# State term on 64x64 tiles, packed states, scores between two psH blocks and a new order, in a fused attention and MLP kernel

## The chip, the cores and the metric

The kernel runs on one NeuronCore of one Trainium2 chip. The metric is the device time of one execution in microseconds (us). A run of the kernel before on the same chip stands beside every run. Where several times are given they are a median, with the lowest and the highest in brackets. A run is called slow when its matmuls ran at a lower pace or it lies over 1.5% above the fastest run of the same kernel; such runs are left out of the ratios.

## The reference

Linear attention with decay, in blocks, then an MLP with ELU. The kernel works on 128 tokens at a time, so 24 blocks ("groups") of 4 sequences by 6 chunks, and computes in f16 with f32 sums.

```python
# q, k, v: (4 sequences, 8 heads, 768 positions, 64); per block of positions:
intra = (q_b @ k_b.T * Dmask) @ v_b              # "scores" S, then the product P with v
inter = (q_b * lam_pow) @ kv_state               # the state term
out_b = intra + inter
kv_state = lam_block * kv_state + (k_b * rev_pow).T @ v_b    # product U, then the update
# x = out as (3072 tokens, 512); w_in (512, 2048), w_out (2048, 512)
h = x @ w_in                                     # first product, psH
g = where(h > 0, h, exp(min(h, 0)) - 1)
y = g @ w_out                                    # second product, psM
```

## The kernel before

Groups 0 to 3 are worked on one by one, the others in pairs. From pair 8 on, the second product is done in seven products of half size in place of eight (a Strassen scheme). It needs sums of neighbouring quarters of g: `fp` (128x512), `fe` (128x256) and `fd` (128x512), and at the end combinations of the seven results (`t`, `u`, `s2`, `w1`). A table says which of the sums go to GpSimd; those are issued at once, the others are queued for VectorE:

```python
SHARED = {8: 'D', 10: 'ED', 12: 'ED', 14: 'ED', 16: '', 18: '', 20: '', 22: 'ED'}
...
for w, out, in0, in1, op in (
    ("P", p, t[:, :, 0], t[:, :, 1], ALU.add),
    ("E", e, t[:, :, 0, 0], t[:, :, 1, 1], ALU.add),
    ("D", d, t[:, :, :, 1], t[:, :, :, 0], ALU.subtract),
):
    if w in SHARED.get(g0, ""):
        nc.gpsimd.tensor_tensor(out=out[:], in0=in0, in1=in1, op=op)
    else:
        todo.append(lambda ...: nc.vector.tensor_tensor(...))
```

In the timelines below every engine works through its instructions in program order (TensorE waits 2.66 us for `pp` with a psM block behind it in its order). Each psH block ends in a "flush", which issues VectorE's `gg` (the last step of g), then one waiting attention piece (`late`, for instance `pp`, the masked scores), then one waiting sum (`slow`):

```python
if late:
    late.pop(0)()
if slow and len(late) < 2:
    slow.pop(0)()
```

The order of a pair is given by a table of positions, counted in psH blocks from the pair's first one: loads of q, k, v (`L`), transposes (`T`), scores (`S`), and the burst of attention products (`B`). GpSimd issues the loads, and its work stands in its own program order: load issues, `fe`, `fd`, `t`, `kd` (the keys with their decay).

```python
AT = {'L': -19, 'l': 1, 'W': -13, 'T': -5, 'S': -7, 'B': -5}
```

Of the kernel before, what the change touches and what calls it, by code (L numbers as in the profile page):

```python
# [15 lines left out]
def kernel(  # L16
# [27 lines left out]
    WI = [2] * 8  # L44
    WO = [2] * 8
    POOL_ORDER = (
        "q1 k0 iota k2 k1 q2 v0 v1 i0 i1 v2 i3 i2 o0 o1 d0 k3 q3 i4 i5 d1 o2 d2 o3 d3 o4 v3 o5 "
        "i6 i7 k4 o7 o6 q4 k6 m4 v4 q6 d5 d4 q8 q10 k8 d6 v6 v8 d7 v10 k10 m6"
# [4 lines left out]
        "z3 z0 z1 Z2 Z1 z2 Z0 T0 T1 S0 S1 T2 P0 P1 S2 1:0:0 U0 1:1:0 P2 1:1:1 1:2:0 2:0:0 "  # L53
        "1:2:1 2:1:0 1:0:1 T3 2:2:0 1:0:2 S3 1:2:2 2:2:1 U1 1:1:2 2:1:1 2:0:1 P3 2:0:2 1:3:0 "
        "2:1:2 1:1:3 M 1:2:3 Z3 2:2:2 1:3:2 U2 1:3:1 2:1:3 1:0:3 T4 T5 2:2:3 1:3:3 S4:5 2:3:0 "
        "2:0:3 2:3:2 U3 F0 B:P4:P5:U4:U5 M 2:3:3 1:4:1 T6 1:4:0 G3 T7 2:3:1 G4 W9 1:4:3 G5 G1 "
        "S6:7 1:4:2 G2 2:5:0 2:4:0 1:4:4 1:4:5 W8 B:P6:P7:U6:U7 1:4:7 1:6:1 2:5:1 2:4:1 G7 "
        "1:4:6 1:6:0 G6 2:4:2 S8:9 1:6:2 1:6:4 2:5:2 2:5:3 W11 1:6:3 1:6:6 B:P8:P9:U8:U9 1:6:7 "
        "2:4:3 1:6:5 W10 L12"
    )  # L60
    LAGU = 13
    LATE = 4
    MACT = 12
    SPLIT = 3
    DELAY = 0
    COMB = nc.gpsimd

    SEVEN = (8, 10, 12, 14, 16, 18, 20, 22)
    SHARED = {8: 'D', 10: 'ED', 12: 'ED', 14: 'ED', 16: '', 18: '', 20: '', 22: 'ED'}
    AT = {'L': -19, 'l': 1, 'W': -13, 'T': -5, 'S': -7, 'B': -5}  # L70
    BANKS = (
        "S0=M0,A S1=D,C S2=D,M1 S3=D,B P0=M1 P1=M0 P2=B P3=A U0=B U1=B U2=B U3=M1 T0=M1,D "
        "T1=D,C T2=M0,D T3=B T4=B T5=D T6=M1 T7=D M2=C M3=M0"
# [19 lines left out]

    stp = [
        [cpool.tile([128, 2, NHP, 128], FP16, name=f"st{x}_{i}") for i in range(2)]
# [5 lines left out]
    def emit_load(w, g0):  # L101
        n = size_of[g0]
        c, b = divmod(g0, B)
        x = {"q": q, "k": k, "v": v}[w]
        src = x[b : b + n, :, c * L : (c + 1) * L].rearrange("b h p d -> p (b h) d")
        t = asb.tile([128, n, H, 64], FP16, tag=f"{w}n{n}", name=f"{w}n{g0}", bufs=4)
        {"q": qg, "k": kg, "v": vg}[w][g0] = t
        nc.gpsimd.dma_start(out=t[:].rearrange("p b h d -> p (b h) d"), in_=src)  # L108
# [38 lines left out]
    def emit_wi(i):  # L147
        written.add(("i", i))
        f0 = sum(WI[:i]) * 128
        nc.gpsimd.dma_start(  # L150
            out=wi16[i][:],
            in_=moe_w_in[:, f0 : f0 + WI[i] * 128].rearrange("(k p) f -> p k f", p=128),
        )
# [48 lines left out]
    def zero_st1(b):  # L202
        nc.vector.memset(st[b][1], 0.0)

# [8 lines left out]

    dn = cpool.tile([128, H], FP32, name="dn")
    mask = cpool.tile([128, H, 128], FP32, name="mask")
    qs = cpool.tile([128, NHP, 128], FP32, name="qs")
    ks = cpool.tile([128, H], FP32, name="ks")
# [11 lines left out]
    for hh in range(2):  # L229
        r = slice(hh * 64, (hh + 1) * 64)  # L230
        nc.vector.tensor_copy(loglam_p[r, :], loglam[r, hh::2])
    nc.vector.tensor_scalar_add(pos[:, 2:3], pos[:, 1:2], float(L))

    def emit_qs():
        for hp in range(NHP):
            nc.scalar.activation(
                qs[:, hp, :], row[:], AF.Exp, scale=loglam_p[:, hp : hp + 1]
            )
# [90 lines left out]

    def att_P(g):  # L330
        cb, b = divmod(g, B)
        until(E_done, g)
        if cb > 0:
            until(Y_done, g - B)
        vt = of(vg, g)
        qt, _ = qkT[g]
        po = bank(f"P{g}", 0, [128, NHP, 128], FP32, f"psO{g}")
        R = [slice(0, 64), slice(64, 128)]
        for hp in range(NHP):
            for hh, r in enumerate(R):  # L340
                nc.tensor.matmul(  # L341
                    po[r, hp, :], lhsT=vt[:, 2 * hp + hh, :], rhs=Pt[(g, hh)][:, hp, :],
                    start=True, stop=(cb == 0), skip_group_check=True,
                )
            if cb > 0:
                for r in R:
                    nc.tensor.matmul(  # L347
                        po[r, hp, :], lhsT=st[b][cb % 2][:, hp, r], rhs=qt[:, hp, :],
                        start=False, stop=True, skip_group_check=True,
                    )  # L350

        def evacuate():
            g0 = GFIRST[g]
            n = GSIZE[g0]
            if g0 not in xg:
                xg[g0] = asb.tile(
                    [128, NHP, n * 128], FP16, tag=f"xt{n}", name=f"xt{g0}",
                    bufs=4 if n == 1 else 2,
                )
            dst = xg[g0][:, :, (g - g0) * 128 : (g - g0 + 1) * 128]  # L360
            if g < GPE:
                nc.scalar.copy(out=dst, in_=po[:])
            else:
                nc.vector.tensor_tensor(out=dst, in0=po[:], in1=qs[:], op=ALU.mult)
            X_done.add(g)

        return [evacuate]

    stt = {}

    def att_M(g):

        cb, b = divmod(g, B)
        if cb == NCB - 1 or b % 2:
            return
        assert {f"U{g - B}", f"U{g - B + 1}"} <= seen
        until(Y_done, g - B)
        until(Y_done, g - B + 1)
        old = stp[b // 2][cb % 2]
        tmp = asb.tile([128, 2, NHP, 128], FP32, tag="stt", name=f"stt{g}", bufs=2)  # L380
        stt[g] = tmp
        if g >= MACT:
            for hp in range(NHP):
                nc.scalar.activation(
                    tmp[:, :, hp, :], old[:, :, hp, :], AF.Copy, scale=upp[:, hp : hp + 1]
                )
            return
        for hh in range(2):
            r = slice(hh * 64, (hh + 1) * 64)
            for x in range(2):  # L390
                nc.gpsimd.tensor_tensor(
                    out=tmp[r, x, :, r], in0=old[r, x, :, r],
                    in1=upp[r].unsqueeze(2).broadcast_to([64, NHP, 64]), op=ALU.mult,
                )
# [5 lines left out]
    def att_U(g, pu=None):  # L400
# [5 lines left out]
        if pu is None:  # L406
            full = bank(f"U{g}", 0, [128, NHP, 128], FP32, f"psU{g}")
            for hp in range(NHP):
                nc.tensor.matmul(
                    full[:, hp, :].rearrange("p (h e) -> p h e", h=2),  # L410
                    lhsT=kds[g][:, 2 * hp : 2 * hp + 2, :],
                    rhs=vt[:, 2 * hp : 2 * hp + 2, :], start=True, stop=True,
                )
        else:
            for hp in range(NHP):
                for hh in range(2):
                    r = slice(hh * 64, (hh + 1) * 64)
                    nc.tensor.matmul(
                        pu[r, hp, :], lhsT=kds[g][:, 2 * hp + hh, :], rhs=vt[:, 2 * hp + hh, :],
                        start=True, stop=True, skip_group_check=True,  # L420
                    )
# [4 lines left out]
        def update(hh):  # L426
            r = slice(hh * 64, (hh + 1) * 64)
            nc.vector.tensor_copy(new[r, :, r], full[r, :, r])
            if hh == 1:
                Y_done.add(g)  # L430
# [3 lines left out]
    def updates(g, pu):  # L434
# [4 lines left out]
        def update(hh):  # L439
            r = slice(hh * 64, (hh + 1) * 64)  # L440
            nc.vector.tensor_tensor(
                out=new[r, :, :, r], in0=stt[g][r, :, :, r], in1=pu[r], op=ALU.add
            )
            if hh == 1:
                Y_done.update((g, g + 1))

        return [lambda: update(0), lambda: update(1)]

    def burst(*ops):

        us = [int(o[1:]) for o in ops if o[0] == "U" and int(o[1:]) // B < NCB - 1]
        evs, i = [], 0
        for o in ops:
            if o[0] == "P":
                evs += att_P(int(o[1:]))
# [67 lines left out]
    def mm2_seven(g0, i):  # L523
# [6 lines left out]
        while slow and i in (2, 4, 5):  # L530
            slow.pop(0)()
# [4 lines left out]
        while i == 6 and "w1" not in z:  # L536
            late.pop(0)()
# [102 lines left out]
        elif m == 1:  # L640
            late.insert(0, lambda: comb("w1", "u", None, ALU.add, nc.vector))
# [10 lines left out]
    def flush():  # L652
        while pending:
# [19 lines left out]
            if g0 in SEVEN and j % 2 == 1:  # L673
                slow.extend(sums(g0, j // 2))
        if late:
            late.pop(0)()
        if slow and len(late) < 2:
            slow.pop(0)()
# [64 lines left out]
    def zero_st(b):  # L743
        nc.scalar.memzero(st[b][0])

# [8 lines left out]
    def ready(t):  # L754
# [4 lines left out]
        if t[0] == "U" and g < 2 * B:  # L759
            assert f"{'z' if g < B else 'Z'}{g % B}" in seen  # L760
# [4 lines left out]
    def run(t):  # L765
# [11 lines left out]
        if w in "PUzZ":  # L777
            ready(t)
        if w == "S":
# [4 lines left out]
            late.pop(0)()  # L784
            late.pop(0)()
# [6 lines left out]
        else:  # L792
            {"T": att_T_pe, "1": mm1, "2": mm2, "Z": zero_st, "z": zero_st1,
             "q": lambda g, e: cast_raw(g, "q", e), "k": lambda g, e: cast_raw(g, "k", e),
             "7": mm2_seven, "F": w_sums, "G": lambda i: w_sums(i, nc.gpsimd), "c": lambda i: (emit_qs, emit_mask, emit_ks)[i](), "W": pool_work,
# [94 lines left out]
```

## Time and profile before

| | before |
|---|---|
| time | 212.09 us (212.03 to 213.15) |
| span of the profiled run | 210.7 us |
| TensorE, VectorE, ScalarE, GpSimd busy | 195.4, 159.0, 138.0, 159.9 us |
| one pair, 96 to 158 us | 15.50 us |

The columns of a line of the costliest groups are the source line, engine and operation, output and input, count, then the busy time in us and the mean of one in ns, and the idle time ahead of it.

```profile
L501 DVE TENSOR_TENSOR fp<-gg 128x512 f16<-128x512 f16 x32 | 14.6, 455 | 0.6
```

The 32 `fp` sums on VectorE take 0.46 us each on average, 0.70 at most.

### The profile page before, as it was taken

What the parts mean: (1) busy time and instruction counts of PE and PEld (TensorE: products, weight loads), DVE (VectorE), ACT (ScalarE), POOL (GpSimd) and SP (SyncE); (2) the same over time, 40 slices, a digit from 0 to 9 for tenths busy, and PEclk for the clock granted to TensorE, in tenths of its full rate; (3) what the DMA queues carried; (4) which work ended last, traced back from release to release, by engine and by line L of the source; (5) the groups of instructions that cost most, each with busy time, mean ns of one, the idle gap of its engine ahead of it and who ended that gap; (6) DMA issues with size and microseconds to landing.
All of it is one profiled execution on the core that took longest, in us unless ns stands there. A gap on an engine that the chain in (4) does not pass through costs nothing.

```text
span 210.7 us, 5654 instructions
## 1 busy us (share of the span) xinstructions
PE 195.4 (93%) x2224; PEld 156.4 (74%) x2224; DVE 159.0 (75%) x294; ACT 138.0 (65%) x277; POOL 159.9 (76%) x187
## 2 busy tenths in 40 slices
PE   0687999999999999999999999999999999999993
PEld 0366776767676776767887887887988888888882
DVE  3774572689956878889979879879989889886632
ACT  4537664874877675867966967867567667667640
POOL 7999799999999999497999999996370301205961
PEclk9999999999999999999999999999999999999999
DMA  7999999999993030999949969979999911011032
GB/s 86 133 165 193 194 195 186 164 184 188 135 179 83 3 100 4 133 165 150 129 88 153 120 99 153 116 93 154 153 79 180 106 51 52 3 50 50 3 121 78
DMA packets 102122, 24.61 MB, mean 117 GB/s; under 512 B 92624, under 2 KB 99280, under 8 KB 102096
## 3 DMA queue, kind: packets, MB, share of 16 engines
q0 software_dynamic: 79760, 13.50, 83.5%
q1 hardware_dynamic: 22336, 10.76, 27.1%
q8 instruction: 17, 0.28, 0.5%
q14 instruction: 9, 0.07, 0.2%
HBM read 27.27 MB, written 6.29 MB: 159 GB/s over the span
## 4 chain that ended last, share of the span: by engine, by line
PE 66%; DVE 9%; POOL 8%; ACT 7%; DMA 4%; issue 3%; ACTq 0%; POOLq 0%; DVEq 0%
PE psH L700 30%; PE psM L567 18%; PE psM L725 11%; DMA wo<-in_moe_w_out_dram 4%; ACT e L706 3%; ACT psH L707 3%; DVE gg L666 3%; PE psS L305 3%; PE psO L341 2%; DVE g L666 2%; PE psO L347 1%; POOL wi L150 1%; POOL fe L498 1%; POOL vn L108 1%; POOL kn L108 1%
## 5 line engine op out<-in xcount | busy, mean ns | idle before, releaser
L700 PE MATMUL psH<-xt,wi 128*128 128x256 f16 (+1 forms) x896 | 99.6, 258 | 2.9 <-DVE gg L666 1.3
L700 PEld LDWEIGHTS <-wi 128*128 128x128 f16 x896 | 77.8, 98 | 17.8 <-issue 4.3
L706 ACT ACTIVATE e<-psH 128x512 f32<-128x512 f32 x96 | 57.3, 597 | 47.0 <-PE psH L700 46.0
L707 ACT ACTIVATE psH<-psH 128x512 f32<-128x512 f32 x96 | 57.0, 593 | 0.0
L666 DVE SCALAR_TENSOR_TENSOR gg<-e,psH 128x512 f16<-128x512 f32 x64 | 43.7, 682 | 15.8 <-ACT psH L707 15.5
L666 DVE SCALAR_TENSOR_TENSOR g<-e,psH 128x512 f16<-128x512 f32 x32 | 21.9, 684 | 17.7 <-ACT psH L707 17.5
L321 DVE TENSOR_TENSOR pp<-psS,mask 128x512 f16<-128x512 f32 x48 | 31.4, 683 | 4.0 <-PE psS L305 4.0
L725 PE MATMUL psM<-wo,g 128*128 128x512 f16 x128 | 32.1, 379 | 0.4 <-DMA wo<-in_moe_w_out_dram 0.3
L498 POOL TENSOR_TENSOR fd<-gg 128x512 f16<-128x512 f16 x20 | 24.3, 1215 | 0.1
L177 POOL TENSOR_TENSOR kd<-kn,ks 128x512 f16<-128x512 f16 x20 | 21.1, 1057 | 4.2 <-DMA kn<-in_k_dram 4.1
L518 POOL TENSOR_TENSOR wf<-wo 128x256 f16<-128x256 f16 (+1 forms) x28 | 21.1, 789 | 0.2
L498 POOL TENSOR_TENSOR fe<-gg 128x256 f16<-128x256 f16 x16 | 11.7, 729 | 12.2 <-DVE gg L666 12.1
L620 POOL TENSOR_TENSOR t<-m,m 128x256 f32<-128x256 f32 x8 | 5.9, 734 | 18.1 <-ACT m L553 18.1
L725 PEld LDWEIGHTS <-g 128*128 128x128 f16 x128 | 11.7, 98 | 10.3 <-issue 0.8
L567 PE MATMUL psM<-wf,gg 128*128 128x256 f16 x128 | 16.7, 273 | 0.1
L567 PE MATMUL psM<-wo,fp 128*128 128x256 f16 x128 | 16.5, 273 | 0.0
L567 PE MATMUL psM<-wf,fd 128*128 128x256 f16 x128 | 16.4, 273 | 0.0
L108 POOL DMA_DIRECT2D qn<-in_q_dram x13 | 14.7, 1135 | 0.9 <-POOLq L874 0.8
L108 POOL DMA_DIRECT2D kn<-in_k_dram x14 | 15.4, 1098 | 0.0
L108 POOL DMA_DIRECT2D vn<-in_v_dram x14 | 15.3, 1099 | 0.0
L501 DVE TENSOR_TENSOR fp<-gg 128x512 f16<-128x512 f16 x32 | 14.6, 455 | 0.6
L567 PEld LDWEIGHTS <-gg 128*128 128x128 f16 x128 | 11.9, 98 | 2.3 <-DVE gg L666 0.4
(62 smaller groups left out, 249.4 us busy)
## 6 DMA issues: line engine op xcount, KB each, us to landing
out_dram<-osb SPq DMA_DIRECT2D x22, 256.0 KB, 2.7
kn<-in_k_dram POOLq DMA_DIRECT2D x10, 256.0 KB, 6.5
qn<-in_q_dram POOLq DMA_DIRECT2D x10, 256.0 KB, 6.3
vn<-in_v_dram POOLq DMA_DIRECT2D x10, 256.0 KB, 8.3
wi<-in_moe_w_in_dram POOLq DMA_DIRECT2D x8, 256.0 KB, 7.5
wo<-in_moe_w_out_dram POOLq DMA_DIRECT2D x8, 256.0 KB, 8.9
kn<-in_k_dram POOLq DMA_DIRECT2D x4, 128.0 KB, 4.5
vn<-in_v_dram POOLq DMA_DIRECT2D x4, 128.0 KB, 5.7
```

Source lines behind the costliest of these rows:

```text
L108: nc.gpsimd.dma_start(out=t[:].rearrange("p b h d -> p (b h) d"), in_=src)
L177: nc.gpsimd.tensor_tensor(out=kd[:], in0=of(kg, g), in1=ks[:].unsqueeze(2).broadcast_to([128, H, 64]), op=ALU.mult,)
L321: nc.vector.tensor_tensor(out=P[:], in0=pts[hh][:], in1=mask[:, hh::2, :], op=ALU.mult)
L498: nc.gpsimd.tensor_tensor(out=out[:], in0=in0, in1=in1, op=op)
L501: lambda out=out, in0=in0, in1=in1, op=op: nc.vector.tensor_tensor(out=out[:], in0=in0, in1=in1, op=op)
L518: eng.tensor_tensor(out=out, in0=in0, in1=in1, op=op)
L567: nc.tensor.matmul(place_of(m), lhsT=lhs, rhs=rhs, start=(s == 0 and m in (3, 4, 1, 7)), stop=(s == NFT // 2 - 1), skip_group_check=True,)
L666: nc.vector.scalar_tensor_tensor(out=g.rearrange("p f c t -> p (f c t)"), in0=e[:], scalar=-1.0, in1=r[:], op0=ALU.add, op1=ALU.min,)
L700: nc.tensor.matmul(pH[:, f * n * 128 : (f + 1) * n * 128], lhsT=wi16[i][:, kk, w * 128 : (w + 1) * 128], rhs=xg[g0][:, kk, :], start=(kk = ...
L706: nc.scalar.activation(e[:], pH[:], AF.Exp)
L707: nc.scalar.activation(pH[:], pH[:], AF.Relu)
L725: nc.tensor.matmul(psM[g][:, cols], lhsT=gts[(g, j * FB + f)], rhs=wo16[i][:, w, cols], start=first and f == 0, stop=end and f == FB - 1, ...
```

## The change

Its intent is to shorten what TensorE does in a pair (state term on four tiles at once), to put the 16 score matmuls where TensorE waits for a psH bank, to drop the zero blocks of the state tiles, and to let a product wait for its own pair's sums alone. The tables of the order were then tuned as a whole. The core of the diff:

```diff
-    WI = [2] * 8
+    WI = [4] * 4                                  # w_in in pieces of 64 partitions x 512 columns
     POOL_ORDER = (
-        "q1 k0 iota k2 k1 q2 v0 v1 i0 i1 v2 i3 i2 o0 o1 d0 ...
+        "q1 k0 k1 k2 iota q2 v1 v0 i0 v2 i1 d0 i3 i2 o0 o1 ...
     OPEN = (
-        "z3 z0 z1 Z2 Z1 z2 Z0 T0 T1 S0 S1 T2 P0 P1 S2 1:0:0 U0 1:1:0 P2 ...
+        "T0 S0 T1 T2 P0 S1 U0 P1 S2 1:0:0 1:1:0 P2 ...
-    COMB = nc.gpsimd
+    COMB = nc.vector
-    SHARED = {8: 'D', 10: 'ED', 12: 'ED', 14: 'ED', 16: '', 18: '', 20: '', 22: 'ED'}
-    AT = {'L': -19, 'l': 1, 'W': -13, 'T': -5, 'S': -7, 'B': -5}
+    SHARED = {8: 'ED', 10: 'ED', 12: 'ED', 14: 'ED', 16: 'ED', 18: '', 20: '', 22: 'ED'}
+    AT = {'L': -18, 'l': 1, 'W': -13, 'T': -7, 'S': -8, 'B': -5}
 ...
-        [cpool.tile([128, 2, NHP, 128], FP16, name=f"st{x}_{i}") for i in range(2)]
+        [cpool.tile([128, 2, NHP, 64], FP16, name=f"st{x}_{i}") for i in range(2)]
 ...
+    def att_P2(g):                                 # state term of a pair, 64x64 tiles
+        for a in range(2):
+            for i in range(2):
+                for c in range(2):
+                    for e in range(2):
+                        nc.tensor.matmul(
+                            po[e][R[c], a, i, :],
+                            lhsT=st[(g + i) % B][cb % 2][R[e], 2 * c + a, :],
+                            rhs=qkT[g + i][0][R[e], 2 * c + a, :], ...)
 ...
-        return [lambda: update(0), lambda: update(1)]
+        def update():
+            nc.vector.tensor_tensor(out=new[:], in0=stt[g][:], in1=pu[:], op=ALU.add)
```

## The prediction

> **What bounds the kernel now.** I read the page first, then the chain of waits in order of time, then the timeline of TensorE and VectorE, and last a table of busy time by stretch.
>
> The page says that TensorE is busy in 93% of a span of 210.7 us, VectorE, GpSimd and ScalarE in 75%, 76% and 65%. So the question is what TensorE executes and where it stands still. The table by stretch, two stretches of it:
>
> ```profile
> core 0: us, PE busy (x) PEld busy (x) DVE busy (x) ACT busy (x) POOL busy (x), PEclk, DMA share, GB/s
> 0.00:21.50 21.50, 12.11 (x142) 9.11 (x143) 12.59 (x28) 11.54 (x26) 19.80 (x29) 1.00 1.50 145
> ...
> 127.00:142.50 15.50, 15.29 (x185) 13.25 (x185) 13.05 (x24) 11.53 (x25) 14.99 (x17) 1.00 1.23 120
> ```
>
> The clock is 1.00. In the second half one pair of blocks costs 15.50 us, and the pairs from 96 to 158 us are alike. There GpSimd has only half a microsecond to spare, VectorE 2.4. The start is another regime; its chain of waits:
>
> ```profile
> 11.80 0.59 POOL wo L158
> 12.39 9.12 DMA wo<-in_moe_w_out_dram
> 21.51 0.04 issue
> 21.55 0.59 PE psM L725 x2
> ```
>
> Until 21.5 us the end of the chain is a weight transfer. What TensorE does before that is hidden.
>
> Inside one pair of the steady part, the timeline of TensorE (start, length, line, operands, count; a group of overlapped matmuls is printed with its last one's drain, so I use differences of starts):
>
> ```profile
> 131.11 1.04 PE L700 MATMUL psH<-xt,wi 128*128 128x256 f16 x8
> 132.07 0.25 PE L341 MATMUL psO<-pp,vn 128*64 128x128 f16 x2
> 132.16 0.22 PE L347 MATMUL psO<-qT,st 128*64 128x128 f16 x2
> ...
> 132.99 0.42 PE L418 MATMUL psU<-vn,kd 128*64 128x64 f16 x16
> 133.34 1.05 PE L567 MATMUL psM<-wo,fp 128*128 128x256 f16 x8
> ...
> 140.34 1.04 PE L567 MATMUL psM<-wf,fd 128*128 128x256 f16 x8
> 141.21 1.04 PE L700 MATMUL psH<-xt,wi 128*128 128x256 f16 x8
> 142.46 1.03 PE L700 MATMUL psH<-xt,wi 128*128 128x256 f16 x8 [0.21 <-DVE gg L666]
> 143.43 0.62 PE L305 MATMUL psS<-qT,kT 64*128 64x128 f16 x16
> 143.98 1.05 PE L567 MATMUL psM<-wf,gg 128*128 128x256 f16 x8
> ```
>
> A dense block of eight takes 0.87 us (140.34 to 141.21). A pair has 8 of the first product (psH) and 7 of the second (psM): 15 x 0.873 = 13.10. The scores take 0.55 plus 0.10 on entry. The attention burst, from 131.98 (131.11 + 0.87) to 133.34, takes 1.36: 0.09 on entry, 0.92 for 32 matmuls, 0.35 for the state products. The block at 141.21 lasts 1.25 until the next: 0.38 lost. Sum 13.10 + 0.65 + 1.36 + 0.38 = 15.49, so the pair is explained. The 0.38 is in the chain of waits:
>
> ```profile
> 140.60 0.60 ACT e L706
> 141.20 0.50 ACT psH L707
> ...
> 141.72 0.70 DVE gg L666
> 142.42 0.04 issue
> 142.46 1.03 PE psH L700 x8
> ```
>
> psH has two banks. The third psH block from now must wait until both activations and the VectorE step of the first have run: 140.34 to 142.46 = 2.12 us after the first one's matmuls. Two psH blocks in a row with one second-product block before them offer only 2 x 0.87 = 1.74.
>
> **What the Trainium skill says.** "TensorEngine Tiling (Array Packing)", Key Properties: changing the tiling mode drains TensorE, while tiles of one mode run independently. The trace agrees: a block before a change lasts 0.96 in place of 0.87, about 0.1 us per change. Its Gotcha 1 says that different row tiles must not use one PSUM bank at the same time; the changed kernel writes the two row halves to two banks, so this is respected. "TensorE: Matmul & The Clock Gate", section "Wait — 56ns, not 53.3ns?", gives a floor of about 25 ns between starts of matmuls. The trace differs for tiles: the 16 of psU start from 133.0 to 133.2 and the block gives way after 0.35 less about 0.12 for the mode change, 0.23/16 = 14 ns each. The measurement decides. "SBUF — State Buffer", Door 1: DMA bandwidth depends on how many of 16 ports the partitions reach, and 64 partitions of one half reach 8. No transfer before shows it; it is a rival below.
>
> **The change, part by part.**
>
> (1) State term on 64x64 tiles. Before, a pair's 16 state matmuls run two at a time on 128 rows of which 64 multiply zeros: 16 x 27.5 ns = 0.44 (32 of both kinds take 0.92 with the first one's 0.04). Four at a time, at the 14 ns just seen, they take 16 x 14 = 0.22. But they now stand in a mode of their own ahead of the products with v, so one mode change of 0.1 is added. Net 0.12 a pair; pairs 4 to 22 are ten: 1.2 us. All on the path.
>
> (2) Scores in the gap. By the order of instructions, the 16 score matmuls now stand between the two neighbouring psH blocks in place of after them. The time offered grows from 1.74 to 1.74 + 0.65 = 2.39, over the 2.12 needed. The 0.38 is gone wherever there are scores: the traces show such a gap at 94.7, 110.2, 125.7, 141.2, 156.7 and 172 us, six times, 2.3 us. The one at 187 stays, as the last pair has no scores after it.
>
> (3) States without zero blocks. VectorE's two state updates (0.68 each, 64 partitions) become one of 128 partitions, 512 elements long as before: 0.68 saved a pair. GpSimd's four scalings of 0.64 become one of about 1.1 (its 128x512 products take 1.06 to 1.2): 1.4 saved for each of the first pairs. ScalarE's four of 0.50 are halved in length. The zero fills (1.1 on VectorE, 1.4 on ScalarE) go. Four activations of 0.39 for a second decay table come to ScalarE, later. All of it is beside the path, except where VectorE is what TensorE waits for.
>
> (4) Two combinations move from GpSimd to VectorE: -2 x 0.73 and +2 x 0.42. VectorE in a steady pair: 13.05 - 0.68 + 0.83 = 13.2, GpSimd 14.99 - 1.47 = 13.5. Both must fit the new period, 15.50 - 0.38 - 0.12 = 15.0. They do. The sums of pairs 8 and 16 go to GpSimd, which sat idle in part there.
>
> (5) The middle, 21 to 95 us. Stalls in the timeline beyond work and mode changes: 0.38 at 34.98 (psH twice in a row), 0.6 at 54.87 (half of the scores wait for kT behind a VectorE queue with 1.65 of weight sums and two state updates), 0.3 at 61.7, 0.38 at 77.09 and 0.3 at 79.21, where VectorE does this:
>
> ```profile
> 77.60 0.69 DVE L666 SCALAR_TENSOR_TENSOR g<-e,psH 128x512 f16<-128x512 f32 x1 [0.63 <-ACT psH L707]
> 78.20 1.40 DVE L441 TENSOR_TENSOR st<-stt,psU 64x512 f16<-64x512 f32 x2
> 79.63 0.69 DVE L666 SCALAR_TENSOR_TENSOR g<-e,psH 128x512 f16<-128x512 f32 x1
> ```
>
> In the new order the pair at 34.98 has other work before it, and one state update in place of two frees 0.7 at 79. The repeat at 77 stays. Of the 1.96 I count 0.38 as sure and half of the other 1.2, 0.6: 1.0 us.
>
> (6) The start. Same bytes stand ahead of the first two w_out pieces. Until they land, both orders have the same four psH blocks behind them. The iota comes two issues later (1.8 us), so the first transposes do too, near 7.5; kT and the mask then set the scores near 9.3 against 9.49 before, and the two first pairs' products reach psH at about 15.8 against 14.4. That still meets the transfer at 21. Zero, give or take 0.5.
>
> (7) The tail is the same 56 matmuls of the last pair and a store of 128 KB: zero.
>
> Sum: 1.2 + 2.3 + 1.0 = 4.5. I add 0.3 for the order, which was retuned as a whole (a choice, not a measurement). 212.1 - 4.8 = 207.3 us.
>
> **The rivals.**
>
> The extra mode changes eat the tiles: if each costs 0.2, or the four tiles don't overlap fully, part 1 is zero or slightly negative. For it: the burst gains a third tiling mode. Against: the three kinds of change in the trace all cost about 0.1. Time: 208.5.
>
> VectorE becomes the bound. It takes over combinations whose inputs come from GpSimd and ScalarE, and it works in order, so a late GpSimd sum would hold back the step that frees psH. For it: pairs 18 and 20 keep all sums on VectorE (13.67 of 15.3 before, 14.5 with the combinations). Against: at 133 us the GpSimd sum was ready two microseconds before VectorE would use it. If it stalls 0.3 a pair: 209.5.
>
> The start slips: w_in in 64-partition pieces reaches half of the ports, or psH starts late for good. For it: DMA engines are above 90% busy from 5 to 47 us. Against: descriptors get twice as long, and the two halves lie on different ports. Time: up to 210.
>
> The other way: fewer and longer w_in descriptors bring w_out earlier, and the new order clears all stalls of the middle: 205.
>
> **Range and chances.** Part 2 is arithmetic on a bank that I can see; parts 1 and 5 may each be off by a microsecond, the start by one either way. That makes 205.2 to 209.4. The line of 2% lies at 207.85, only 0.55 above my number, so faster by over 2% gets 0.62, within 2% 0.36, slower 0.02.
>
> **What would show it.** A steady pair of 15.0; the score block between two psH blocks with no wait behind it; state matmuls starting 14 ns apart, some 0.25 for sixteen; one state update of 0.68; the first w_out product still near 21 us. I am wrong if the pair stays at 15.5, if VectorE's wait for GpSimd shows up ahead of psH, or if the second product begins after 22 us.

## The result

| | before | changed |
|---|---|---|
| time, same rounds | 212.24 us (212.03 to 213.15) | 223.41 us (221.22 to 225.07, the last a slow run) |
| span of the profiled run | 210.7 us | 221.7 us |
| PE, DVE, ACT, POOL busy | 195.4, 159.0, 138.0, 159.9 us | 197.1, 165.3, 135.6, 152.5 us |

The changed kernel is correct and slower, by a ratio of 1.0483 (95% interval 1.04 to 1.0567). A ratio is the mean time of one kernel's fast runs over that of the other's fast runs of the same rounds, so it is not quite the ratio of the medians.

The table of busy time by stretch, of which the prediction showed the row for 127 to 142.5 us before, has this row in the changed kernel (length, then busy time and number of instructions of TensorE, its weight loads, VectorE, ScalarE, GpSimd; granted clock, DMA share, GB/s):

```profile
127.00:142.50 15.50, 11.59 (x134) 9.65 (x133) 14.44 (x21) 9.54 (x21) 11.70 (x13) 1.00 1.11 119
```

TensorE is busy for 11.59 in place of 15.29 us, VectorE for 14.44 in place of 13.05 with fewer instructions (21, not 24). So VectorE's instructions have become longer, and TensorE waits.

VectorE was to save 0.68 us in a pair, less what the combinations add, yet its busy time rose by 6.3 us. The groups of the changed kernel name the row:

```profile
L545 DVE TENSOR_TENSOR fp<-gg 128x512 f16<-128x512 f16 x32 | 26.0, 813 | 0.6
```

The same 32 sums of the same size now last 813 ns on average in place of 455. The median is still about 0.42 us; four of them last 3.82, 3.01, 3.80 and 2.82 us. Here is the first of the four in the timelines of VectorE, GpSimd and TensorE of the changed kernel (start, length, engine, line, operation):

```profile
101.40 0.69 DVE L337 TENSOR_TENSOR pp<-psS,mask 128x512 f16<-128x512 f32 x1
102.00 3.82 DVE L545 TENSOR_TENSOR fp<-gg 128x512 f16<-128x512 f16 x1
105.74 0.68 DVE L337 TENSOR_TENSOR pp<-psS,mask 128x512 f16<-128x512 f32 x1
```

```profile
100.87 1.19 POOL L110 DMA_DIRECT2D vn<-in_v_dram  x1
102.07 0.69 POOL L542 TENSOR_TENSOR fe<-gg 128x256 f16<-128x256 f16 x1
102.70 1.16 POOL L542 TENSOR_TENSOR fd<-gg 128x512 f16<-128x512 f16 x1
103.81 0.72 POOL L662 TENSOR_TENSOR t<-m,m 128x256 f32<-128x256 f32 x1
104.50 1.03 POOL L186 TENSOR_TENSOR kd<-kn,ks 128x512 f16<-128x512 f16 x1
```

```profile
106.48 0.36 PE L359 MATMUL psO<-pp,vn 128*64 128x128 f16 x6 [2.66 <-DVE pp L337]
```

VectorE starts `fp` while GpSimd ends the issue of a v load. GpSimd then runs four sums without a break, to 104.50 + 1.03 = 105.53, and `fp` ends at 105.82, 0.29 us later. The other three end 0.28 to 0.29 us after the end of such a run as well. A sum of 0.42 us has in effect waited for the whole run. Three of the four start 1.13 to 1.15 us after the start of a v load's issue; the second, at 125.36, starts 4.76 us after one, in the middle of a run that has gone on without a break since that load. So the sum need not stand right behind the load. Behind it in VectorE's order stands `pp`, and behind `pp` the attention products of TensorE, which waits 2.66 us. "The Trainium skill", page "SBUF — State Buffer", section "SBUF: two separate sides", calls the port pair that VectorE and GpSimd share "an exclusive lock, not a bandwidth split", held for the whole instruction. That covers a wait for one GpSimd sum, 0.7 to 1.2 us here. It does not say that VectorE can lose several boundaries in a row, as it does here after `fe`, `fd` and `t`.

The start changed as well. In the kernel before, the chain of waits went through a w_out transfer up to 21.51; in the changed kernel it goes through a piece of w_in (start, length, what):

```profile
9.55 7.75 DMA wi<-in_moe_w_in_dram
...
17.34 3.61 PE psH L742 x32
```

The first psH block starts at 17.34 in place of 14.42, the second product at 23.74 in place of 20.87.

By differences of the starts of the scores, against the same kernel without the long sums (run e11 below), TensorE lost 4.5 us around the first long sum, 1.5 at the second (there it waits for `u`, not for `pp`), 2.8 at the third and 1.8 at the fourth: 10.6 us of the 11.0 by which 221.7 exceeds 210.7. The first cost more than its wait of 2.66, because the matmuls after it ran slowly; the granted clock was 0.50 there (columns as above):

```profile
107.00:110.00 3.00, 3.00 (x23) 2.13 (x18) 2.73 (x6) 0.37 (x1) 1.64 (x2) 0.50 0.83 181
```

After the third, with a wait of 2.63 us, it stayed at 1.00. What the prediction counted on is then either small or cancelled by something else. Both had to be tested.

### The profile page after: what moved, and what is told of

It reads as the page before. It is cut to its first block, busy times and chain, and to the rows that moved or that the text cites. A ratio compares the mean times of both kernels' runs of the same rounds, so it can differ in the third digit from the quotient of the medians.

```text
span 221.7 us, 5620 instructions
## 1 busy us (share of the span) xinstructions
PE 197.1 (89%) x2224; PEld 156.4 (71%) x2224; DVE 165.3 (75%) x288; ACT 135.6 (61%) x277; POOL 152.5 (69%) x171
## 4 chain that ended last, share of the span: by engine, by line
PE 64%; DVE 15%; ACT 6%; issue 5%; POOL 5%; DMA 3%; POOLq 0%; ACTq 0%; DVEq 0%
PE psH L742 31%; PE psM L609 17%; PE psM L767 9%; DVE fp L545 5%; DMA wi<-in_moe_w_in_dram 3%; DVE pp L337 3%; ACT e L748 2%; DVE gg L708 2%; ACT psH L749 2%; PE psO L359 2%; PE psS L321 2%; POOL vn L110 1%; POOL kn L110 1%; DVE wf L562 1%; DVE g L708 1%
## 5 line engine op out<-in xcount | busy, mean ns | idle before, releaser
L742 PE MATMUL psH<-xt,wi 128*128 128x256 f16 (+1 forms) x896 | 101.3, 262 | 1.2 <-DVE g L708 0.6
L708 DVE SCALAR_TENSOR_TENSOR gg<-e,psH 128x512 f16<-128x512 f32 x64 | 43.7, 683 | 15.8 <-ACT psH L749 15.3
L542 POOL TENSOR_TENSOR fe<-gg 128x256 f16<-128x256 f16 x24 | 18.0, 750 | 38.3 <-DVE gg L708 38.0
L337 DVE TENSOR_TENSOR pp<-psS,mask 128x512 f16<-128x512 f32 x48 | 32.2, 684 | 3.3 <-PE psS L321 3.3
L767 PE MATMUL psM<-wo,g 128*128 128x512 f16 x128 | 31.6, 379 | 0.0
L542 POOL TENSOR_TENSOR fd<-gg 128x512 f16<-128x512 f16 x24 | 28.6, 1191 | 0.0
L545 DVE TENSOR_TENSOR fp<-gg 128x512 f16<-128x512 f16 x32 | 26.0, 813 | 0.6
L359 PE MATMUL psO<-pp,vn 128*64 128x128 f16 x192 | 9.7, 233 | 8.9 <-DVE pp L337 7.5
L609 PE MATMUL psM<-wo,fp 128*128 128x256 f16 x128 | 17.3, 282 | 0.0
```

The lines of the kernel that those rows point to most:

```text
L337: nc.vector.tensor_tensor(out=P[:], in0=pts[hh][:], in1=mask[:, hh::2, :], op=ALU.mult)
L545: lambda out=out, in0=in0, in1=in1, op=op: nc.vector.tensor_tensor(out=out[:], in0=in0, in1=in1, op=op)
L609: nc.tensor.matmul(place_of(m), lhsT=lhs, rhs=rhs, start=(s == 0 and m in (3, 4, 1, 7)), stop=(s == NFT // 2 - 1), skip_group_check=True,)
L708: nc.vector.scalar_tensor_tensor(out=g.rearrange("p f c t -> p (f c t)"), in0=e[:], scalar=-1.0, in1=r[:], op0=ALU.add, op1=ALU.min,)
L742: nc.tensor.matmul(pH[:, f * n * 128 : (f + 1) * n * 128], lhsT=wi16[i][:, kk, w * 128 : (w + 1) * 128], rhs=xg[g0][:, kk, :], start=(kk = ...
L767: nc.tensor.matmul(psM[g][:, cols], lhsT=gts[(g, j * FB + f)], rhs=wo16[i][:, w, cols], start=first and f == 0, stop=end and f == FB - 1, ...
```

## The experiments

All edits are to the changed kernel unless said. All results are correct except those of the two sweeps, which compute something else.

### Which part makes the long sums

**e1_late_first**: `fp` waits until no attention piece is queued.

```diff
-        if slow and len(late) < 2:
+        if slow and not late:
```

> One condition changed: a pair's sum on VectorE is only taken when no other deferred VectorE step is waiting, so the fp sum follows the last pp step in place of standing before it. It then starts about 0.6 us into GpSimd's fe, not at the moment in which fe starts. Theory A (fp is shut out of SBUF by a run of GpSimd sums that begins at the same moment): no fp over 1 us is left, the 11 us that TensorE lost at four places are gone, 212 us, one pair 15.0. Rival B (VectorE has too much to do, or waits for the combinations it took over): nothing moves, 223 us.

214.88 us (214.78 to 215.72), ratio 1.0096 (1.0043 to 1.0148). One sum of 3.22 us remains, three last 1.72 to 1.76. So most of the loss goes when the sum meets GpSimd elsewhere and `pp` is ahead of it.

**e2_no_pool_sums**: `fe` and `fd` of pairs 8 to 20 on VectorE.

```diff
-    SHARED = {8: 'ED', 10: 'ED', 12: 'ED', 14: 'ED', 16: 'ED', 18: '', 20: '', 22: 'ED'}
+    SHARED = {8: '', 10: '', 12: '', 14: '', 16: '', 18: '', 20: '', 22: 'ED'}
```

> The fe and fd sums of all pairs but the last go to VectorE. Theory A: GpSimd has no run of sums to shut fp out, so no fp over 1 us; VectorE has 2.8 us more in a pair, 15.6 to 16 against 15.0, so 214 to 217 us. Rival B (VectorE overloaded): slower than the changed kernel, 226 us or more.

The fast runs took 215.71 to 217.94 us, ratio 1.0167 (1.0099 to 1.0235), near the 214 to 217 us of theory A. One run took 504.95 us with the matmuls slow throughout; its cause was not looked for. It is also the one that was profiled. No `fp` is long in that trace (412 to 427 ns), but at its pace the engines meet differently, so for the absence of long sums in the fast runs there are only the times.

**e3_comb_pool**: the combinations back on GpSimd.

```diff
-    COMB = nc.vector
+    COMB = nc.gpsimd
```

> Only the two combinations go back to GpSimd. Theory A: the four long fp stay, since the run of GpSimd sums behind fe is the same or longer, so 221 us or more. Rival B (the combinations on VectorE are the cause): back to 212 us.

219.24 us (217.68 to 219.98), ratio 1.028 (1.0222 to 1.0338); long sums of 3.83, 2.77 and 2.81 us remain, three in place of four. The combinations are not the cause, though their place shifts what is caught.

**e4_scores_after**: scores after the second psH block, as before.

```diff
-    AT = {... 'S': -8, ...}
+    AT = {... 'S': -7, ...}
```

> Only the place of the scores of pairs from 10 on goes back, behind the second psH block. Theory A: VectorE's order is that of the kernel before, fp meets fe 0.37 us after its start, no long fp, but the 0.38 us gap returns about five times: 223.4 - 11 + 2 = 214 us. Rival B: no recovery, 225 us.

227.35 us (225.41 to 232.98), ratio 1.064 (1.057 to 1.071), with sums of 3.51, 3.75, 3.49 and 2.50 us. The profiled run was a slow one; the long sums alone are read from it. The scores' new place is not the cause either, and without it the kernel is slower still.

**e8_fp_at_once**: `fp` is issued straight after its `gg`, ahead of `pp`.

```diff
-                slow.extend((g0, x) for x in sums(g0, j // 2))
+                fresh = sums(g0, j // 2)
+                fresh.pop(0)()
+                slow.extend((g0, x) for x in fresh)
```

> The fp sum is taken at once behind the VectorE step gg that it and GpSimd's fe both need, so it always stands at VectorE before fe is released. All theories of the lock: fp as in the trials where fe came 0.04 to 0.11 us after it, 0.42 us, no wait over 1 us, the 11 us of the four places gone: 212 us. Rival B (VectorE has too much to do): 223 us.

215.13 us (214.06 to 217.47, the last a slow run), ratio 1.009 (1.0045 to 1.0134). One sum of 3.26 us is left, which starts during `kd`, 4.4 us after the start of a v load's issue. Moving `fp` helps as much as e1, from the other side; what counts is where it falls against GpSimd.

**e9_fp_old_pool**: e8 with the whole load list of before.

> The same with the list of GpSimd's loads of the kernel before (iota two loads earlier, v0 ahead of v1, v2 behind both pieces of w_in). The traces have the first psH block at 17.34 us against 14.42 and the first second-product block at 23.74 against 20.87; if the order of loads makes that, both come back to within 1 us of before and the time is 2 us under that of the run with fp at once, 210 us. If the half-partition pieces of w_in make it, no more than 0.5 us.

Three runs took 234.85 to 236.1 us, one 214.83. In the profiled one, slow, the group of four VectorE sums over w_out that starts at 52.10 lasts 20.94 us (one of them 14.06) beside a long row of GpSimd's own, and one `fp` lasts 3.27. So `fp` is not special: another f16 sum can be caught too. The run decides nothing about the list.

### The lock by itself

**e7_sweep**: a kernel of its own. In 64 trials GpSimd runs sums like `fe`, `fd`, `t` and `kd` back to back; VectorE starts one f16 sum of 128x512, each time 25 ns later.

> A kernel by itself, wrong in its result on purpose: 64 trials, in each of which GpSimd runs four sums one behind the other (f16 256, f16 512, f32 256, f16 512) and VectorE, released by the same ScalarE step, runs PSUM products of a length that grows by 25 ns a trial and then one f16 sum out of SBUF like fp. Theory A1 (a sum of VectorE waits for every GpSimd sum already handed to its engine): the later it comes, the more sums it waits for, always to the end of one of them plus 0.29 us; waits over 1 us at many offsets. Theory A2 (it only loses where it meets the start of a GpSimd sum within some 0.07 us, and then loses to the end of the run): long waits in narrow bands of one to five trials, else it gets in at the end of the current sum. Theory A3 (plain lock): never longer than the rest of one sum, at most 1.5 us.

317.02 us. In 63 of the 64 trials the sum gets in at the end of the GpSimd sum that was running and ends 0.27 to 0.37 us after it; in the other one both start together and VectorE goes first. The longest, as the timelines of VectorE and GpSimd show it:

```profile
110.46 1.34 DVE L65 TENSOR_TENSOR fp<-src 128x512 f16<-128x512 f16 x1
```

```profile
110.36 1.15 POOL L54 TENSOR_TENSOR fd<-src 128x512 f16<-128x512 f16 x1
```

`fp` ends at 111.80, 0.29 after the end of `fd`; the next GpSimd sum, `t`, takes 0.90 in place of 0.72, as it has to wait in its turn. This is the plain lock of the skill's page. It does not make 3.8 us.

**e10_sweep_dma**: the same with the issue of a load on GpSimd ahead of the four sums, in 60 trials with steps of 50 ns.

> The sweep again (60 trials, wrong result on purpose), with a load of GpSimd ahead of the four sums, as v comes ahead of fe in the changed kernel, and steps of 50 ns. Without a load the VectorE sum always got in at the end of the current GpSimd sum, 1.34 us at most. Theory H (behind a load, GpSimd does not let VectorE in between sums that follow each other without a gap): at most offsets the sum ends 0.29 us after the last GpSimd sum, waits up to 3.9 us. If the load does nothing: ends 0.29 us after the current one as before, at most 1.5 us, and the long waits of the kernel need another cause.

373.43 us. Counted from the start of the load's issue, sums that start at 0.97 to 1.82 get in after `fe`. Those that start at 1.86 to 2.91, while `fd` runs, do not get in after it but only after `t`:

```profile
160.42 2.11 DVE L69 TENSOR_TENSOR fp<-src 128x512 f16<-128x512 f16 x1
```

```profile
160.41 1.15 POOL L58 TENSOR_TENSOR fd<-src 128x512 f16<-128x512 f16 x1
161.52 0.72 POOL L59 TENSOR_TENSOR t<-s 128x256 f32<-128x256 f32 x1
```

`fp` ends at 162.53, 0.29 after `t` ended at 162.24, and past the end of `fd` at 161.56. In the first trial it lost two boundaries and waited 2.74 us, for `kd`. So behind a load's issue a boundary can be lost, and without one none was. But theory H had expected waits to the end of the run at most offsets; 19 of the 60 trials lost the boundary after a sum, 18 of them only one, and none waited 3 us. The 3.8 us of the kernel were not made by themselves. What decides which boundary is lost stays open: in this sweep a sum that starts 1.13 us after the issue gets in after `fe`, in the changed kernel one that starts 1.13 after it (102.00 less 100.87) loses all.

### The one number

**e11_loads_earlier**: the loads one psH block earlier, as before. Nothing else.

```diff
-    AT = {'L': -18, 'l': 1, 'W': -13, 'T': -7, 'S': -8, 'B': -5}
+    AT = {'L': -19, 'l': 1, 'W': -13, 'T': -7, 'S': -8, 'B': -5}
```

> The changed kernel with one number put back: the loads of a pair are issued one psH block earlier, so the v load no longer stands right ahead of the fe that meets fp. Theory H: GpSimd falls idle between the load and that fe, and the long fp of the changed kernel go at least at three of four places: 213 to 216 us. If loads have nothing to do with it: 222 us or more.

212.65 us (212.12 to 214.25), ratio 0.9989 (0.9943 to 1.0035). No `fp` is long. The same sum of the same pair, in the timelines of VectorE and GpSimd of this run:

```profile
101.99 0.51 DVE L545 TENSOR_TENSOR fp<-gg 128x512 f16<-128x512 f16 x1
```

```profile
98.05 1.15 POOL L110 DMA_DIRECT2D vn<-in_v_dram  x1
...
101.55 0.67 POOL L542 TENSOR_TENSOR fe<-gg 128x256 f16<-128x256 f16 x1 [0.56 <-DVE gg L708]
102.18 1.34 POOL L542 TENSOR_TENSOR fd<-gg 128x512 f16<-128x512 f16 x1
```

It starts at 101.99, as in the changed kernel at 102.00. The load of v is out of the way since 99.2, GpSimd stood idle for 0.56 ahead of `fe`, and `fp` gets in between `fe` and `fd`: 0.51 us in place of 3.82. The number is worth 223.41 - 212.65 = 10.8 us, all of the loss against before. In the changed kernel's profiled run the loss includes the stretch at a clock of 0.50; in this run the clock is 1.00.

**e14_before_l18**: the kernel *before*, with the number moved the other way.

```diff
-    AT = {'L': -19, ...}
+    AT = {'L': -18, ...}
```

> The kernel before, with one number of its order moved the other way: the loads of q, k and v one step later, as in the changed kernel. Theory A (the one number suffices, whatever else the order is): long sums of 2.5 us or more appear on VectorE, and the time rises by several us, 215 to 224. Theory B (the number does harm only together with the rest of the new order, because what counts is where a sum of VectorE happens to fall against an unbroken run of GpSimd sums behind a load): no sum above 1.5 us and 212 to 214. I lean to B with 0.6: in the kernel before, the combinations follow other sums on GpSimd and its runs are broken elsewhere.

219.41 us (218.54 to 220.21), ratio 1.0318 (1.0279 to 1.0356). I leaned to the wrong side. The old kernel gets the same long sums, of 3.81 and 2.55 us, from that number alone. The first of them in VectorE's timeline:

```profile
115.68 3.81 DVE L501 TENSOR_TENSOR fp<-gg 128x512 f16<-128x512 f16 x1
```

A v load's issue started on GpSimd at 114.54, so again `fp` starts 1.14 us after such a start, and TensorE waits 2.67 us for `pp` behind it. So the new order is not needed for it; it has more such places (four in place of two).

**e12_fp_loads**: e11 and e8 together.

> Both: fp at once behind gg, and the loads one block earlier. No fp over 1 us; against the run with fp at once alone (one place of 3.3 us left) 3 us less: 211.5 to 213 us. What remains above 210.5 is the start, 2.9 us later than before at the first second-product block.

212.95 us (212.22 to 213.79), ratio 0.9992 (0.9952 to 1.0032); the longest `fp` lasts 1.07 us. Once no sum is caught for longer, its place in the queue is worth nothing.

### Where the gain went

**e16_scores_after_l19**: e11 with the scores after the second psH block.

```diff
-    AT = {'L': -19, ... 'S': -8, ...}
+    AT = {'L': -19, ... 'S': -7, ...}
```

> The changed kernel with the loads one step earlier (212.65), and the scores after the second psH block as in the kernel before. Part 2 of the prediction valued the scores in the gap at 0.38 us for each of some six pairs: so 2.3 us more, 214.9, with a wait of 0.21 and a start-to-start of 1.25 on the second psH block again. Rival (the gap is worth nothing because VectorE delays the same block in any case): 212.7. A second rival: a changed order brings long sums back, and the time goes above 217.

218.52 us (217.36 to 219.12), ratio 1.0257 (1.0219 to 1.0294), with no `fp` above 1.09 us. A pair takes 16.05 us (scores start at 116.49, 132.54 and 148.59), in e11 15.03. Two places in TensorE's timeline make up the 1.02:

```profile
131.58 1.03 PE L742 MATMUL psH<-xt,wi 128*128 128x256 f16 x8 [0.21 <-DVE gg L708]
...
137.97 0.36 PE L359 MATMUL psO<-pp,vn 128*64 128x128 f16 x6 [0.46 <-DVE pp L337]
```

The first is the gap that the prediction named (1.25 from start to start, 0.38 lost). The second it did not name: with the scores later, `pp` comes later too, and the burst, with its wait, takes 0.65 longer. In e11 neither wait is there. But ahead of that `pp` VectorE runs an `fp` that was held by GpSimd:

```profile
135.63 1.09 DVE L545 TENSOR_TENSOR fp<-gg 128x512 f16<-128x512 f16 x1
```

It ends 0.28 us after GpSimd's `fd` (135.28 to 136.44). In e11 the same sum takes 0.51, and 0.58 less is more than the wait of 0.46. So the lock has a share in this cost too, and the 1.02 is not all owed to the place of the scores.

**e15_tail**: e11 with the last pair's `t` on VectorE.

```diff
-            nc.gpsimd.tensor_tensor(
+            (nc.vector if last else nc.gpsimd).tensor_tensor(
                 out=z["t"][:], in0=z["m3"][:], in1=z["m4"][:], op=ALU.add
```

> The changed kernel with the loads one step earlier (212.65), and for the last pair alone the sum t = m3 + m4 on VectorE in place of GpSimd. Theory of the tail: the product block at 204.93 waits 0.52 us for u, u waits for t, and t stands on GpSimd behind two sums of the last hidden slice; with t on VectorE the wait goes: 0.5 us less, 212.1, and no wait on that block. Rival: the wait passes to the store or to ScalarE's copies: nothing, 212.65.

212.55 us with one slow run of 216.93 (fast ones 211.52 to 213.09), ratio 0.9974 (0.9941 to 1.0006). The wait of the block behind it falls from 0.52 to 0.20 us, and the block before it takes 2.11 in place of 2.43. So the mechanism is right; of the 0.5 expected, 0.3 came in the trace.

**e6_before_wi64**: the kernel *before* with w_in in pieces of 64 partitions and 512 columns.

```diff
-    WI = [2] * 8
+    WI = [4] * 4
...
-            in_=moe_w_in[:, f0 : f0 + WI[i] * 128].rearrange("(k p) f -> p k f", p=128),
+            in_=moe_w_in[:, f0 : f0 + WI[i] * 128].rearrange(
+                "(k h p) f -> h p k f", h=2, p=64
+            )[hf],
```

> The kernel before with w_in loaded in pieces of 64 partitions and 512 columns in place of 128 partitions and 256 columns, everything else kept. If such pieces land later, 213 to 215 us and the first psH block past 15 us; if the shape doesn't matter, 212 to 212.6 us.

213.43 us (212.67 to 213.62), ratio 1.002 (0.9989 to 1.005). The first psH block starts at 14.88 in place of 14.42, the second product at 21.71 in place of 20.87. The shape of the pieces makes a part of the late start (0.46 of 2.92 and 0.84 of 2.87 us) and not the most; in the whole time it does not show.

**e13_fp_loads_start**: e12 with the head of the load list changed (iota third, v0 ahead of v1) and one set of weight sums moved to GpSimd.

> The same with the head of the load list as before the change (iota early, v0 ahead of v1, v2 behind both pieces of w_in) and the fourth weight sum on GpSimd in place of VectorE. If the head of the list makes the late start, the first psH block comes back to 14.4 to 15 us and the time is 1.5 to 2.5 us under the run without it: 209 to 211 us, under the kernel before. If not, no more than 0.5 us.

219.12 us (217.3 to 221.31), ratio 1.0252 (1.0192 to 1.0312). The profiled run was slow and shows a row of GpSimd's weight sums at 60 to 77 us in the chain of waits, and a caught `fp` of 4.04. Two edits in one run were a mistake: it says nothing clean of the start.

**e17_start**: e11 with the head of the load list alone.

```diff
-        "q1 k0 k1 k2 iota q2 v1 v0 i0 v2 i1 d0 i3 i2 o0 o1 k3 ...
+        "q1 k0 iota k1 k2 q2 v0 i0 i1 v1 v2 d0 i3 i2 o0 o1 k3 ...
```

> The changed kernel with the loads one step earlier (212.65); only the head of the load list is changed: iota in third place, v0 ahead of v1, both halves of the first w_in piece directly after v0. Theory of the start (the order of the loads makes the 2.75 us by which the first psH block is late, 17.17 against 14.42): first psH block between 14.5 and 15.5, second product at 21 to 22, time 210.5 to 211.5. Rival (the two halves land no earlier, because the DMA engines are shared by what is in flight; or TensorE's slow first matmuls eat it): psH at 16.4 or later, time 212.3 to 213. Risk: other alignment, a long sum comes back.

212.91 us with one slow run of 217.68 (fast ones 211.5 to 213.67), ratio 0.9987 (0.995 to 1.0024). The first psH block starts at 17.80, no earlier: in TensorE's order the products with v1 stand ahead of it, and v1 landed at 16.64.

**e18_start2_tail**: e17 with the tail of e15, and the first psH block ahead of those products.

```diff
-        "T0 S0 T1 T2 P0 S1 U0 P1 S2 1:0:0 1:1:0 P2 ...
+        "T0 S0 T1 P0 S1 T2 1:0:0 P1 S2 U0 1:1:0 P2 ...
```

> The run with the early w_in piece showed what holds the start: the products of the second block with v (P1) stand ahead of the first psH block in TensorE's order, and v1 landed at 16.64 us, 8.24 after its issue. Here, on top of that load list and of the tail edit, the first psH block stands ahead of P1. If the order of instructions is what makes the start late: first psH block at 14.5 to 15.5 us, second product at 21.5 to 22.5, a time of 211.0, ratio 0.992. Rival (the start is bound by the bytes on their way and by TensorE's slow first matmuls, whatever the order): the second product stays at 23 to 24 and the time at 212.0 to 212.6.

212.67 us (211.09 to 213.17), ratio 0.9982 (0.995 to 1.0013). The first psH block now starts at 15.21, 2 us earlier, and the second product still at 23.43 (e11: 23.27, before: 20.87). TensorE's timeline, first of the kernel before, then of this run, shows why:

```profile
16.07 1.06 PE L700 MATMUL psH<-xt,wi 128*128 128x128 f16 x16
17.29 0.41 PE L341 MATMUL psO<-pp,vn 128*64 128x128 f16 x8 [0.17 <-DVE st L428]
```

```profile
15.21 1.87 PE L742 MATMUL psH<-xt,wi 128*128 128x128 f16 x16 [1.90 <-DMA wi<-in_moe_w_in_dram]
17.00 0.64 PE L359 MATMUL psO<-pp,vn 128*64 128x128 f16 x8
...
18.76 1.86 PE L742 MATMUL psH<-xt,wi 128*128 128x128 f16 x16
20.55 0.62 PE L359 MATMUL psO<-pp,vn 128*64 128x128 f16 x8
```

Eight products with v take 0.41 in the kernel before at 17.29, and 0.62 here at 20.55; a block of 16 takes 1.06 with its drain against 1.86. TensorE ran at full pace from about 16 us in the kernel before, and only after some 21 us here. Two blocks took 1.79 from start to start, where the fast ones take 0.87: 1.84 us lost. The kernel before had one slow block (1.42: 0.55 lost). So the pace of these blocks makes about 1.3 of the 2.56 us by which the second product is late; the small products between them ran slowly too, and a third block lost 0.36 waiting for VectorE's `g`. The kernel before waits 1.21 us for w_in and w_out in the same stretch, so this is no closed account. "The Trainium skill", page "TensorE: Matmul & The Clock Gate", Part 1, says that TensorE starts at half its clock and is released after a window of about 3.4 us in which it was busy. That fits: in the kernel before TensorE works from 9.49 to 17.13 with one wait of 0.61 us, in this run it stood idle for 1.76 and 1.90 us in that time, in the changed kernel for 1.44. e6 has two waits of 0.61 us in that stretch and runs its psH block of 16 at 16.99 slowly. But the granted clock of all these traces reads 1.00 up to 23 us, so it does not show the slow pace, and no run here warms TensorE alone. This cause is argued and not shown.

**e19_start3_tail**: e18 with a second psH block ahead of the products with v1.

```diff
-        "T0 S0 T1 P0 S1 T2 1:0:0 P1 S2 U0 1:1:0 P2 1:1:1 1:2:0 2:0:0 2:1:0 1:2:1 1:0:1 T3 ...
+        "T0 S0 T1 P0 S1 T2 1:0:0 1:0:1 P1 S2 U0 1:1:0 P2 1:1:1 1:2:0 2:0:0 2:1:0 1:2:1 T3 ...
```

> The same, with two psH blocks of the first token block ahead of P1, both from the first w_in piece, so that the wait for v1 is filled too. If TensorE's order is the cause: the second product at 21 to 22 us, a time of 210.6, ratio 0.990. Rival as above: 212.0 to 212.6, because the second product then waits for w_out, which lands at 21.5 us in the kernel before and later here, as its issue stands behind more loads. A risk for both: other alignment against GpSimd's runs brings a long sum back, 3 us for each.

215.28 us (215.13 to 215.76), ratio 1.0127 (1.0106 to 1.0149). My premise was wrong: one psH block already uses all of the first w_in piece, so the second block needs the next one and waits for it to 20.08 (3.01 us). The second product then starts at 27.69. No version found beats the kernel before beyond the uncertainty of the runs.

## Why the prediction was wrong

It said 207.3 us; the kernel takes 223.41. The 16.1 us have two sources.

**The rival "VectorE becomes the bound", and the durations behind it.** The step that failed is "VectorE in a steady pair: 13.05 - 0.68 + 0.83 = 13.2", with durations taken over from the old trace, and a rival that knew one kind of wait only, that for a late GpSimd sum as data, at 0.3 a pair. Its only term for the new order was a gain of 0.3. A sum of 0.42 became one of 3.8 because of *when* it was issued against a load and a run of GpSimd sums, and it held back `pp`, not "the step that frees psH". e11 shows the size, 10.8 us, and that one number of the order brings it about; e14 shows it in the old kernel; the times of e2 agree that GpSimd's sums are needed for it. The number stood in the diff, and the prediction did not weigh it. The old trace had a small sign: the `fp` at 130.96 lasts 0.58 us in place of 0.42 and ends 0.28 after GpSimd's `fe` (130.59 + 0.67), as the caught ones do. With it undone, VectorE's busy time in a pair (113.00 to 128.13) is 12.95, near the 13.2; GpSimd's is 14.10, 0.6 over the 13.5 that was worked out.

**The 5.3 us that are left** (212.65 less 207.3) follow from e11's trace, by the lag of the same point of work behind the kernel before. The lag is 2.40 us at the second product; 1.93 after the score block and both psH blocks around it at 97 us; -0.32 at the same point five pairs later; +0.37 at the last `fe` block. Term by term:

- Part (6), the start, "Zero, give or take 0.5": it cost 2.4 us. The first psH block was expected at about 15.8 and came at 17.17, and its matmuls ran at half pace until 20, which the prediction did not count at all. The prediction's own sign of being wrong, a second product after 22 us, came true (23.74, in e11 23.27). The rival "the start slips" had the right place; of its two reasons the pieces of w_in make a part at most (0.84 us at the second product in e6), and psH does start late.
- Parts (1) and (2), the pair: right. Predicted 15.0, measured 15.03 (113.00 to 128.13 and on: 15.13, 15.03, 15.04); five pairs gave 1.93 + 0.32 = 2.25 us. The score block stands between the psH blocks with no wait behind it, here in e11:

```profile
128.13 0.62 PE L321 MATMUL psS<-qT,kT 64*128 64x128 f16 x16
128.69 1.05 PE L742 MATMUL psH<-xt,wi 128*128 128x256 f16 x8
```

  The 16 state matmuls take 0.34 to 0.35 with their mode change, so 0.21 to 0.22 and 0.13, as worked out, and the rival on mode changes falls. What part (2) is worth may be understated: without it a pair of the new order takes 1.02 more (e16), of which 0.38 is the gap and the rest the later `pp`, in part behind a held `fp`.
- Part (3) was right in size on VectorE (one update of 0.68) and lies beside the path of a steady pair. ScalarE's four scalings fell from 0.50 to 0.39 each and not to half.
- Part (5), the middle, was to give 1.0, with its share of parts (1) and (2) and 0.3 for the order on top. From the second product to 97 us only 2.40 - 1.93 = 0.5 came. From 52.26 VectorE's four sums over w_out take 2.98 us beside a GpSimd run, and TensorE, which waits for the state update behind them, loses 0.5 there; where the rest went was not followed.
- Part (7), the tail, "zero": it cost 0.37 + 0.32 = 0.7 us. The block ahead of the last takes 2.43 in e11 and 1.75 before; the next one waits for VectorE's `u`, which waits for GpSimd's `t` behind `fe` and `fd`. e15 takes 0.3 of it away.

The sum is 2.40 - 0.5 - 2.25 + 0.7 = +0.4 us, which is the difference of the two spans, 211.1 and 210.7. So the parts of the change that act in a pair do what they should, and the start and the end give it back.

What stays open: why a sum of VectorE loses some boundaries and not others, and how much of the late start is TensorE's pace.

## What to carry to other kernels

A duration from a trace holds only for the neighbours that it had: where VectorE and GpSimd both run sums out of SBUF, look at the longest of a group and not at its mean, and ask what a moved load or sum will then meet. When a retuned order is slower, search its numbers one by one before the large parts of the change: here one integer made 10.8 us and hid that everything else was even. And price the first 20 us on their own, with the pace that TensorE has there.

## What the Trainium skill lacked or had wrong

- "SBUF — State Buffer" gives the port pair that VectorE and GpSimd share as a lock held for one instruction. The sweep without a load agrees (a sum ends 0.27 to 0.37 us after the GpSimd sum that was running, 1.34 us at most). It lacks that VectorE can lose several boundaries in a row when GpSimd's sums follow a load's issue without a break: up to 2.74 us in the sweep with a load, 3.82 us and four sums in the changed kernel.
- "SBUF — State Buffer", Door 1, expects 64 partitions to reach half of the ports. The kernel before with w_in in such pieces took 1.002 times as long (0.9989 to 1.005), and a piece landed 7.8 us after its issue in place of 7.5 (medians). So no halving shows here; but no run times one transfer alone, so the page is not contradicted.
- "TensorE: Matmul & The Clock Gate" gives about 25 ns as the least distance of two starts. The state matmuls on 64x64 tiles start 13 to 14 ns apart (16 in 0.21 to 0.22 us). This is no error of the page, whose Part 3 counts only about 4 ns for each further packed tile, and the prediction passed over that; what it lacks is the pace of a row of matmuls on four such tiles.
- The same page puts the cost of the slow first stretch below 1% of a typical span. Nothing here contradicts it: the slow psH blocks of e18 make about 1.3 us against the kernel before, 0.6% of the span, and that the clock gate is their cause was argued and not shown.
